# A first MLP tile of 768 tokens in two parts that share each chunk of weights

## The chip, the cores and the metric

The kernel runs on 1 core of one Trainium2 chip. The metric is the device time of one execution in microseconds. The core's engines are TensorE (PE; PEld in the profile is its weight load), VectorE (DVE), ScalarE (ACT), GpSimd (POOL) and SyncE (SP), each with a queue of instructions that it works through in order; matmul results go to PSUM, which has 8 banks of 128 x 512 fp32.

## The reference

All is fp32. Attention with a decay bias over 8 batches, 8 heads, 576 positions; then, on its output x, a Fourier mixing, a layer norm and an MLP of 512 to 2048 to 512:

```python
scores = q @ k.T / sqrt(D); bias = -(cum[:, None] - cum[None, :])   # cum: running sum of max(s, 0)
scores = where(causal, -1e9, scores + minimum(bias, 0))
x = softmax(scores) @ v                       # heads side by side: [8, 576, 512]
u = x + real(fft(fft(x, axis=1), axis=2))     # over positions, then over features
un = (u - mean(u)) / sqrt(var(u) + 1e-6)
out = u + relu(un @ w_ch1) @ w_ch2            # 512x2048, 2048x512
```

## The kernel before

**Attention.** The 32 pairs of heads (8 batches of 4) go through a loop, `for i in range(NP)`, in which the steps of several pairs are woven together: scores of pair i, `av` of pair i - 1, `recip` and `finish` of pair i - 2. `recip` sends the softmax sums through DRAM and back as a broadcast `rb`; `finish` multiplies and, for half of the pairs, moves the result into `xs` by DMA. When a batch's four pairs are finished, `folds` adds and subtracts mirrored halves on DVE, ACT and POOL, and `fourier` does the mixing in matmuls (pzs, pzc, pyc, pys, p), adds it to xa and xs and writes u to a DRAM buffer `uD`. The Fourier buffers are the pool `fft`.

**The MLP.** The 4608 tokens are cut into 9 tiles of 512 (`TOK`), with features on the partitions. `ln_tile` (L127 on) loads u, takes mean and variance by matmuls with a matrix of ones (`spread_sum`), and leaves the centred values as a rounded high part `uch` and a low part `ucl`, with `mu` and the reciprocal `r` of the deviation. `mlp_tile` (L164 on) goes over 16 chunks f of 128 hidden features. A chunk takes 12 matmuls into a PSUM tile h (`uch` and `ucl` against the chunk's high and low weights wh and wl, L183), a relu that is evicted as zh (ACT, L187) and zl (DVE, L188), and 12 matmuls into four accumulators acc0 to acc3 (L196 to L198), which are issued one chunk later. The tile's outputs are scaled and added up on DVE and POOL through three `o` buffers and one `w` (L204 to L212) and written (L213).

**The weights.** They come as 8-byte floats. `rounded` (L74 on) makes fp32 out of 256 columns in four DVE operations, one ACT and one POOL operation; `load_w` (L101 on) then splits them into wh and wl. Chunks 0 to 5 are converted during attention and parked in DRAM (`wD`); 6 to 15 are converted while the first MLP tile runs, by the generator `rest`, from which `mlp_tile` pulls two chunks ahead and which `ahead` also advances. Chunks 0 to 2 lie in the pool `w0`, 3 to 7 in `w1`, and 8 to 15 in `wB`, which takes the place of the Fourier buffers: `rest` first runs the last batch's mixing to its end and closes `fft`. After that all 16 chunks stay in SBUF for the other 8 tiles.

**Order.** `weave` interleaves generators: it advances the one whose progress (what it has yielded over its total) is smallest. PE keeps the traced order as long as the context `order` is open; for the other engines, and for PE after `order.close()`, the scheduler of the language sets each queue's order at build time, with the traced order as priority.

**PSUM.** `ps` has 3 banks, which `bank` hands out in turn for h, scores, Fourier and sums; `psm` has 5 for attention, and when attention ends `accp` takes four for acc0 to acc3.

**Around the first tile** the order traced is: `av` of the last pair woven with batch 6's mixing, the first tile's layer norm and the loads of chunks 0 to 2; `recip` and `finish` of the last pair; `folds` of the last batch; then the first tile, woven with `fourier` of the last batch and `ahead`. The second tile's layer norm follows with a delay of 9 steps.

Of the kernel before, what the change touches and what calls it, by code (L numbers as in the profile page):

```python
# [8 lines left out]
F32 = mybir.dt.float32  # L9
F32R = mybir.dt.float32r  # L10
AF = mybir.ActivationFunctionType
ALU = mybir.AluOpType
# [14 lines left out]
TOK = 512  # L27
NC = 6
# [13 lines left out]
def fused_kernel(ctx, tc, qkT, vA, sP, wP, tabD, tabS, corr, out):  # L42
# [84 lines left out]
    def ln_tile(t0, n, lag):  # L127
# [10 lines left out]
        mlp = mlps[t0 // TOK % 2]  # L138
        mu = mlp.tile([128, TOK], F32, tag="mu", name="mu")
        nc.scalar.copy(mu[:, :n], pm[:, :n])  # L140
        uch = mlp.tile([128, 4, TOK], F32R, tag="uch", name="uch")
        ucl = mlp.tile([128, 4, TOK], F32R, tag="ucl", name="ucl")
# [14 lines left out]
        r = mlp.tile([128, TOK], F32, tag="r", name="r")  # L157
# [6 lines left out]
    def mlp_tile(t0, n):  # L164
        uch, ucl, mu, r = LN.pop(t0)
        last = t0 + n == NT
        if last:
            w = lnp.tile([128, 4, TOK], F32, tag="u", name="u")
            for j in range(4):
                nc.gpsimd.tensor_add(w[:, j, :n], uch[:, j, :n].bitcast(F32), ucl[:, j, :n].bitcast(F32))  # L170
                nc.gpsimd.tensor_add(w[:, j, :n], w[:, j, :n], mu[:, :n])
        acc = [accp.tile([128, TOK], F32, tag=f"acc{j}", name=f"acc{j}") for j in range(4)]
        held = []
        for f in range(NF + 1):
            if f < NF:
                while min(f + 2, NF) not in W and next(feed, None) is not None:
                    pass
                wh, wl = W[f]
                h = bank("h")
                i = 0  # L180
                for a, b in ((wh, uch), (wl, uch), (wh, ucl)):
                    for j in range(4):
                        nc.tensor.matmul(h[:, :n], a[:, j * 128:(j + 1) * 128], b[:, j, :n], start=i == 0, stop=i == 11)  # L183
                        i += 1
                zh = zp.tile([128, TOK], F32R, tag="zh", name="zh", bufs=2)
                zl = zp.tile([128, TOK], F32R, tag="zl", name="zl", bufs=2)
                nc.scalar.activation(zh[:, :n], h[:, :n], AF.Relu)  # L187
                nc.vector.scalar_tensor_tensor(out=zl[:, :n], in0=h[:, :n], scalar=0.0, in1=zh[:, :n].bitcast(F32), op0=ALU.max, op1=ALU.subtract)  # L188
            if f < NF:
                held.append((wh, wl, zh, zl, f))  # L190
            if f and not (last and f == NF - 1):
                steps = [(x, j) for x in range(len(held) if f == NF else 1) for j in range(4)]
                for x, j in sorted(steps, key=lambda s: 2 * s[0] + s[1]):
                    a, b, y, z, g = held[x]
                    cs = slice(512 + j * 128, 512 + (j + 1) * 128)
                    nc.tensor.matmul(acc[j][:, :n], a[:, cs], y[:, :n], start=g == 0, stop=False)  # L196
                    nc.tensor.matmul(acc[j][:, :n], b[:, cs], y[:, :n], start=False, stop=False)  # L197
                    nc.tensor.matmul(acc[j][:, :n], a[:, cs], z[:, :n], start=False, stop=g == NF - 1)  # L198
                del held[0]
            if f < NF:  # L200
                yield 1.0
        for j in range(4):
            o = op.tile([128, TOK], F32, tag="o", name="o", bufs=3)
            nc.vector.tensor_mul(o[:, :n], r[:, :n], acc[j][:, :n])  # L204
            if last:
                nc.vector.tensor_add(w[:, j, :n], w[:, j, :n], o[:, :n])
                o = w[:, j]
            else:
                w = op.tile([128, TOK], F32, tag="w", name="w")
                nc.gpsimd.tensor_add(w[:, :n], uch[:, j, :n].bitcast(F32), ucl[:, j, :n].bitcast(F32))  # L210
                nc.gpsimd.tensor_add(w[:, :n], w[:, :n], mu[:, :n])
                nc.gpsimd.tensor_add(o[:, :n], o[:, :n], w[:, :n])  # L212
            (nc.scalar if last and j % 2 else nc.sync).dma_start(out=out[j, :, t0:t0 + n], in_=o[:, :n])  # L213

# [132 lines left out]
    psm = attb_ctx.enter_context(tc.tile_pool(name="psm", bufs=5, space=PSUM))  # L347
# [229 lines left out]
    tiles = [(t, min(TOK, NT - t)) for t in range(0, NT, TOK)]  # L577
# [7 lines left out]
    for i in range(NP):  # L585
# [26 lines left out]
        if i == NP - 1:  # L612
# [3 lines left out]
            norm = ln_tile(*tiles[0], 6)  # L616
# [3 lines left out]
        if i >= 7 and i % 4 == 3:  # L620
# [17 lines left out]
    accp = ctx.enter_context(pool("accp", space=PSUM))  # L638
    order.close()
# [25 lines left out]
    for x, (t0, n) in enumerate(tiles):  # L665
        streams = [[mlp_tile(t0, n), NF]]
        if x == 0:
            streams.append([chain(idle(1000), mixing), FOURIER * 0.6])
            streams.append([ahead(), 100])
        if x + 1 < len(tiles):  # L670
            streams.append([later(ln_tile(*tiles[x + 1], 1), 4 if x else 9), 12])
        weave(*streams)
# [140 lines left out]
```

## Time and profile before

| | |
|---|---|
| median of 3 runs | 1427.62 us (1426.01 to 1429.96) |
| the profiled execution: time, span | 1426.1 us, 1424.4 us |
| mean granted TensorE clock | 0.971 |
| busy: PE, DVE, ACT, POOL | 1305.1, 745.7, 539.3, 561.6 us |
| first MLP matmul, first matmul of the second tile | at 572.44, at 702.47 us |
| DMA | 125.05 MB, 88 GB/s in the mean |

Times are from the start of the span. A row of the timeline has the start, the length, the engine, the line, the operation, its tiles (out<-in), shapes and count; in square brackets stands the idle time before it and what ended that. Recorded lengths of matmuls overlap, since they are pipelined: what one costs in a row of them is read from start to start. A row by stretch has the stretch, its length, and the busy time of PE, PEld, DVE, ACT and POOL with their counts, then the granted clock, the share of DMA and GB/s. A row of the groups has the line, engine, operation, tiles, shapes and count, then busy us and mean ns of one, then the idle time before.

### The profile page before, as it was taken

The page shows a single profiled execution, that of the slowest core. Times are in us where ns is not written, and L with a number is a line of the kernel's source. Part 1 is how long each engine was busy: PE and PEld are TensorE (multiplying, and loading weights), DVE is VectorE, ACT ScalarE, POOL GpSimd, SP SyncE. Part 2 cuts the span into 40 slices and gives each one's busy share as a digit, 9 for nine tenths or more (in the row PEclk, how much of TensorE's full clock was granted, in tenths as well). Part 3 has the DMA queues.
Part 4 walks back from the last instruction along what each step waited for, and adds up shares of the span by engine and source line. Part 5 has one row for each costly group of instructions (what it writes and reads, how often), then busy time and mean ns, then how long its engine had stood idle before and what let it go on. Part 6 is the DMA issues. An engine that isn't in the chain of part 4 may idle for free.

```text
span 1424.4 us, 17997 instructions
## 1 busy us (share of the span) xinstructions
PE 1305.1 (92%) x6190; PEld 1068.7 (75%) x6190; DVE 745.7 (52%) x1684; ACT 539.3 (38%) x1211; POOL 561.6 (39%) x543
## 2 busy tenths in 40 slices
PE   4887979897988887997899999999999999999998
PEld 3766868686777676775688888888888888888886
DVE  6667677877777788799833233222332223322212
ACT  4775756676665656344321121211212112121110
POOL 6445465656546566565720402204022040123300
PEclk9998999999999997999899999999999999999999
DMA  8555556565655555433200000000000000000000
GB/s 214 156 159 144 163 149 180 158 168 159 159 161 144 166 149 163 162 123 121 79 8 30 31 30 15 15 30 31 30 15 15 30 30 30 15 16 0 30 0 30
DMA packets 78230, 125.05 MB, mean 88 GB/s; under 512 B 11256, under 2 KB 36249, under 8 KB 78139
## 3 DMA queue, kind: packets, MB, share of 16 engines
q1 hardware_dynamic: 75627, 119.83, 28.4%
q0 software_dynamic: 1696, 2.50, 0.9%
q10 hardware_dynamic: 816, 1.57, 0.3%
q8 instruction: 49, 0.80, 0.2%
q14 instruction: 42, 0.34, 0.1%
HBM read 76.85 MB, written 23.07 MB: 70 GB/s over the span
## 4 chain that ended last, share of the span: by engine, by line
PE 51%; DVE 7%; POOL 2%; DMA 1%; issue 1%; ACT 1%; SPq 0%; DVEq 0%; POOLq 0%; ACTq 0%
PE h L183 25%; PE acc L198 8%; PE acc L196 8%; PE acc L197 8%; POOL we L89 1%; DVE wm L88 1%; DVE we L83 1%; DVE wm L85 1%; DVE we L87 1%; DVE wl L114 1%; ACT wh L112 1%; DMA wl<-wD 0%; POOL wl L114 0%; DVE ucl L148 0%; DVE zl L188 0%
## 5 line engine op out<-in xcount | busy, mean ns | idle before, releaser
L188 DVE SCALAR_TENSOR_TENSOR zl<-h,zh 128x512 fp32r<-128x512 f32 x144 | 98.6, 686 | 405.5 <-ACT zh L187 405.4
L187 ACT ACTIVATE zh<-h 128x512 fp32r<-128x512 f32 x144 | 85.9, 596 | 530.1 <-PE h L183 530.1
L198 PE MATMUL acc<-zl,wh 128*128 128x512 f32 x576 | 227.5, 396 | 4.9 <-DVE zl L188 4.9
L196 PE MATMUL acc<-zh,wh 128*128 128x512 f32 x576 | 227.6, 395 | 1.0 <-ACT zh L187 1.0
L197 PE MATMUL acc<-zh,wl 128*128 128x512 f32 x576 | 226.8, 394 | 0.0
L523 PE MATMUL pavB<-P,va 128*128 128x320 f32 (+2 forms) x640 | 189.1, 389 | 9.5 <-ACT stage L527 8.9
L459 PE MATMUL pm<-KQ 128*128 128x256 f32 (+3 forms) x384 | 156.5, 427 | 44.4 <-DVE Mx L466 23.1
L495 ACT ACTIVATE P<-ps 128x320 f32<-128x320 f32 (+4 forms) x384 | 145.9, 393 | 110.5 <-PE ps L492 106.8
L491 PE MATMUL ps<-KQ 128*128 128x256 f32 (+2 forms) x384 | 154.1, 404 | 24.4 <-ACT P L495 14.0
L183 PE MATMUL h<-uch,wh 128*128 128x512 f32 x576 | 159.9, 398 | 8.3 <-ACT wh L112 8.3
L183 PE MATMUL h<-uch,wl 128*128 128x512 f32 x576 | 158.1, 396 | 0.8 <-DVE wl L114 0.8
L183 PE MATMUL h<-ucl,wh 128*128 128x512 f32 x576 | 156.9, 393 | 0.0
L466 DVE CUSTOM_DVE_ANT_0 trash<-pm,amask 128x128 bf16<-128x128 f32 (+3 forms) x256 | 123.5, 482 | 34.2 <-PE pm L459 16.9
L212 POOL TENSOR_TENSOR o<-o,w 128x512 f32<-128x512 f32 x32 | 41.8, 1305 | 252.3 <-issue 218.5
L183 PEld LDWEIGHTS h<-uch,wh 128*128 128x128 f32 x576 | 108.2, 190 | 35.9 <-ACT wh L112 12.1
L198 PEld LDWEIGHTS acc<-zl,wh 128*128 128x128 f32 x576 | 108.7, 189 | 32.0 <-DVE zl L188 6.9
L183 PEld LDWEIGHTS h<-uch,wl 128*128 128x128 f32 x576 | 109.2, 190 | 26.6 <-DVE wl L114 1.2
L196 PEld LDWEIGHTS acc<-zh,wh 128*128 128x128 f32 x576 | 108.6, 188 | 26.1 <-ACT zh L187 1.8
L183 PEld LDWEIGHTS h<-ucl,wh 128*128 128x128 f32 x576 | 108.9, 189 | 24.7
L197 PEld LDWEIGHTS acc<-zh,wl 128*128 128x128 f32 x576 | 108.6, 189 | 24.7
L459 PEld LDWEIGHTS pm<-KQ 128*128 128x128 f32 x384 | 78.4, 207 | 64.7 <-DVE Mx L466 30.2
L492 PE MATMUL ps<-q,k 128*128 128x256 f32 (+2 forms) x384 | 120.5, 316 | 3.1 <-POOL q L438 3.1
(140 smaller groups left out, 2066.9 us busy)
## 6 DMA issues: line engine op xcount, KB each, us to landing
qk<-in_qkT_dram SPq DMA_DIRECT2D x32, 576.0 KB
raw<-in_wP_dram SPq DMA_DIRECT2D x64, 256.0 KB
va<-in_vA_dram SPq DMA_DIRECT2D x32, 480.0 KB
q<-KQ SPq DMA_DIRECT2D x32, 288.0 KB
k<-KQ SPq DMA_DIRECT2D x32, 288.0 KB
rb<-rd SPq DMA_DIRECT2D x64, 144.0 KB
u<-uD SPq DMA_DIRECT2D x8, 1024.0 KB
out_dram<-o SPq DMA_DIRECT2D x32, 256.0 KB
```

Of the source, the lines that this page charges most:

```text
L183: nc.tensor.matmul(h[:, :n], a[:, j * 128:(j + 1) * 128], b[:, j, :n], start=i == 0, stop=i == 11)
L187: nc.scalar.activation(zh[:, :n], h[:, :n], AF.Relu)
L188: nc.vector.scalar_tensor_tensor(out=zl[:, :n], in0=h[:, :n], scalar=0.0, in1=zh[:, :n].bitcast(F32), op0=ALU.max, op1=ALU.subtract)
L196: nc.tensor.matmul(acc[j][:, :n], a[:, cs], y[:, :n], start=g == 0, stop=False)
L197: nc.tensor.matmul(acc[j][:, :n], b[:, cs], y[:, :n], start=False, stop=False)
L198: nc.tensor.matmul(acc[j][:, :n], a[:, cs], z[:, :n], start=False, stop=g == NF - 1)
L459: nc.tensor.matmul(p[:, :n], qy[:, h, 128 * c:128 * c + 128], ky[:, h, k0:k0 + n], start=True, stop=True)
L466: nc.vector.tensor_tensor_reduce(out=trash[:nq, :n], in0=p[:nq, :n], in1=amask[:nq, m0:m0 + n], scale=1.0, scalar=first if x else NEG, op0 ...
L491: nc.tensor.matmul(p[:, :n], ky[:, h, ksl], qy[:, h, a:a + n], start=True, stop=False)
L492: nc.tensor.matmul(p[:, :n], k1[:, h, ksl], q1[:, h, a:a + n], start=False, stop=True)
L495: nc.scalar.activation(P[:, o:o + a + n - lo], p[:, lo - a:n], AF.Exp, scale=0.125)
L523: nc.tensor.matmul(p[:, a - lo:n], va[:, c, vs], P[:, o:o + w], start=c == 0, stop=c == cs[-1])
```

## The change

Tile 0 now has two parts: tokens 0 to 511, and `EXTRA` = 256 more (512 to 767) that use the same chunk of weights two chunks later (`LAG`). The tiles behind it are seven of 512, and a last one of 256. `mlp_tile` takes a list of parts; the work of one chunk of one part is moved into `chunk`, and the output into `write`, without a change in its operations.

The second part has its own `mu`, `uch`, `ucl`, `r` in the pool `mlp0`, its own zh and zl in a pool `zx`, and two PSUM banks `accx`, each of which holds two accumulators of 256 columns. So in tile 0 PSUM holds acc (4 banks), accx (2) and `ps1` (2 banks for h, Fourier and sums, where 3 stood). After tile 0, accx is closed and `ps2` takes its two banks; `bank` then alternates between both pools.

`order.close()` moves ahead of the last pair's `recip` and `finish`, and the first chunk of tile 0 is traced there, with the second part's layer norm; the last batch's `folds` are traced within tile 0, right ahead of `fourier`, behind the third step. The last constant shrinks the SBUF space that is set aside for the descriptors of DMAs issued by POOL, which are the loads of the Fourier tables alone.

```diff
+EXTRA = 256
...
-    ps = ctx.enter_context(tc.tile_pool(name="ps", bufs=3, space=PSUM))
+    ps_ctx = ExitStack()
+    banks = [ps_ctx.enter_context(tc.tile_pool(name="ps", bufs=3, space=PSUM))]
     def bank(name):
-        return ps.tile([128, 512], F32, tag="bank", name=name)
+        banks.append(banks.pop(0))
+        return banks[-1].tile([128, 512], F32, tag="bank", name=name)
...
+    LAG = 2
-    def mlp_tile(t0, n):
+    def mlp_tile(parts):
+        last = sum(parts[-1]) == NT
+        part = []
+        for x, (t0, n) in enumerate(parts):
+            if x:
+                two = [accx.tile([128, 512], F32, tag=f"accx{j}", name=f"accx{j}") for j in range(2)]
+                acc = [two[j // 2][:, 256 * (j % 2):256 * (j % 2) + 256] for j in range(4)]
+            else:
+                acc = [accp.tile([128, TOK], F32, tag=f"acc{j}", name=f"acc{j}") for j in range(4)]
+            part.append(dict(t0=t0, n=n, x="x" if x else "", w=EXTRA if x else TOK, lag=LAG * x, acc=acc, held=[]))
+        for g in range(NF + 1 + LAG * (len(parts) - 1)):
+            if g < NF:
+                while min(g + 2, NF) not in W and next(feed, None) is not None:
+                    pass
+            for p in part:
+                f = g - p["lag"]
+                if 0 <= f <= NF:
+                    chunk(p, f, last)
+            if g < NF:
+                yield 1.0
+        for p in part:
+            yield from write(p, last)
...
-    tiles = [(t, min(TOK, NT - t)) for t in range(0, NT, TOK)]
+    tiles = [[(0, TOK), (TOK, EXTRA)]] + [[(t, min(TOK, NT - t))] for t in range(TOK + EXTRA, NT, TOK)]
...
+    ps_ctx.close()
+    accp = ctx.enter_context(pool("accp", space=PSUM))
+    banks[:] = [ctx.enter_context(tc.tile_pool(name="ps1", bufs=2, space=PSUM, reuse_waits="tile"))]
+    accx_ctx = ExitStack()
+    accx = accx_ctx.enter_context(pool("accx", space=PSUM))
+    zx = ctx.enter_context(pool("zx"))
+    order.close()
+    b = NB - 1
+    feed = iter(())
+    first = mlp_tile(tiles[0])
     recip(NP - 1)
-    finish(NP - 1)
-    b = NB - 1
-    weave([folds(b, *xbuf[b]), 1.0])
-    mixing = fourier(b, *xbuf.pop(b))
+    weave([ln_tile(*tiles[0][1], 2), 10], [take(first, N0 - 2), 1], [later(call(finish, NP - 1), 1), 10])
     attb_ctx.close()
...
-    accp = ctx.enter_context(pool("accp", space=PSUM))
-    order.close()
+    folding = folds(b, *xbuf[b])
+    mixing = chain(folding, fourier(b, *xbuf.pop(b)))
...
-    for x, (t0, n) in enumerate(tiles):
-        streams = [[mlp_tile(t0, n), NF]]
+    for x, parts in enumerate(tiles):
+        streams = [[mlp_tile(parts) if x else first, NF]]
         if x == 0:
             streams.append([chain(idle(1000), mixing), FOURIER * 0.6])
             streams.append([ahead(), 100])
+        if x == 1:
+            accx_ctx.close()
+            banks.append(ctx.enter_context(tc.tile_pool(name="ps2", bufs=2, space=PSUM, reuse_waits="tile")))
...
-    nc = bacc.Bacc("TRN2", target_bir_lowering=False, num_devices=1)
+    nc = bacc.Bacc("TRN2", target_bir_lowering=False, num_devices=1, dynamic_dma_scratch_size=4096)
```

More of the change, by code (lines that the diff above doesn't have):

```diff
@@ L162, in fused_kernel @@
     LN, W = {}, {}
-    def mlp_tile(t0, n):
[L165 to L168, printed above, removed]
-            for j in range(4):
[L170 to L201, printed above, removed]
@@ L202, in mlp_tile, with write @@
+    def write(p, last):
+        t0, n, acc = p["t0"], p["n"], p["acc"]
+        uch, ucl, mu, r = p["ln"]
         for j in range(4):
@@ L213, in mlp_tile @@
             (nc.scalar if last and j % 2 else nc.sync).dma_start(out=out[j, :, t0:t0 + n], in_=o[:, :n])
+        yield 0.0
     fft_ctx = ExitStack()
@@ L615, in fused_kernel @@
             mlps = [ctx.enter_context(pool("mlp0"))]
-            norm = ln_tile(*tiles[0], 6)
+            norm = ln_tile(*tiles[0][0], 6)
             streams.append([take(norm, 10), 10 / 0.9])
```

51 lines of the change are left out of this document (42 added, 9 removed).

## The prediction

> **What bounds the kernel now.** I read the page's slices first, then busy time by stretch, then what TensorE waited for in the first MLP tile, then that tile in order of time.
>
> ```profile
> PE 1305.1 (92%) x6190; PEld 1068.7 (75%) x6190; DVE 745.7 (52%) x1684; ACT 539.3 (38%) x1211; POOL 561.6 (39%) x543
> PE   4887979897988887997899999999999999999998
> DVE  6667677877777788799833233222332223322212
> ...
> PEclk9998999999999997999899999999999999999999
> ```
>
> A slice is 35.6 us. From slice 20 on TensorE is full and VectorE idles: there only fewer matmul columns would help. Slices 16 to 19 (570 to 712 us) are the other way round, VectorE full and TensorE not. That is the first MLP tile, whose chunks of weights are still being made from their 8-byte form. By stretch (busy us and count of PE, PEld, DVE, ACT, POOL; PE clock; DMA):
>
> ```profile
> 640.00:688.00 48.00, 37.44 (x139) 26.50 (x139) 46.60 (x110) 23.76 (x53) 26.30 (x31) 0.95 0.33 110
> 688.00:703.00 15.00, 11.76 (x35) 8.68 (x35) 12.83 (x16) 5.27 (x10) 12.15 (x10) 0.73 0.21 70
> 572.44:702.47 130.03, 110.92 (x473) 85.38 (x472) 116.56 (x247) 56.13 (x125) 77.47 (x84) 0.95 0.36 122
> 702.47:1418.80 716.33, 716.30 (x3102) 582.43 (x3100) 205.91 (x269) 125.73 (x213) 154.76 (x115) 1.00 0.06 22
> ...
> PE h L183 <- ACT wh L112: 8.3, 8, 1.7
> PE acc L198 <- DVE zl L188: 4.9, 4, 2.7
> ...
> DVE xr L559 <- DMA rb<-rd: 3.0, 1, 3.0
> DVE Aw L251 <- DMA xs<-xr: 2.1, 1, 2.1
> ```
>
> Behind the stretches stand waits: two of TensorE in 572 to 703 (us in total, times, longest) and two of VectorE in 572 to 640. TensorE waits for the next chunk's wh, and for a zl that stands behind weight work in VectorE's queue. VectorE is busy 46.60 of 48 us while TensorE issues 139 matmuls. The price of TensorE's work in that tile:
>
> ```profile
> 711.64 1.10 PE L183 MATMUL h<-uch,wh 128*128 128x512 f32 x4
> 717.20 1.10 PE L183 MATMUL h<-uch,wh 128*128 128x512 f32 x4
> ...
> 608.23 0.87 PE L284 MATMUL pzs<-dsin,Do 128*96 128x256 f32 x6
> 608.93 0.88 PE L292 MATMUL pzc<-dcos,De 128*96 128x258 f32 x6
> ...
> 618.18 1.37 PE L315 MATMUL pys<-ssin,zs 96*128 96x290 f32 x9
> 619.39 1.35 PE L336 MATMUL p<-scos,z 97*4 97x290 f32 x9
> ```
>
> Start to start (717.20 - 711.64), a 512-token chunk of 24 matmuls is 5.56 us when nothing waits, so 16 are 89. Six 256-wide matmuls are 0.70 us, 117 ns each; nine 290-wide ones 1.21 us. The last batch's Fourier part (three pzs at 0.70, three pzc at about 0.84, five groups at 1.2) is 10.6 us. With 0.5 of sums the tile is 100 us of work in 130.0: **30 us lost**. That is all that can be filled here.
>
> **The change part by part.**
>
> *256 tokens move from the MLP's steady part into the first tile.* Steady, before: 8 tiles in 716.33 us, 89.54 each. After: 7 tiles, 626.8, and one of 256 tokens: 384 matmuls at 117 ns and 0.5 of sums, 45.4; together 672.2. **Saved behind the first tile: 44.1 us.** The narrow price with whole 128x128 weights, from attention:
>
> ```profile
> 543.90 0.28 PE L492 MATMUL ps<-q,k 128*128 128x256 f32 x1
> 544.02 0.28 PE L491 MATMUL ps<-KQ 128*128 128x256 f32 x1
> 544.14 0.28 PE L492 MATMUL ps<-q,k 128*128 128x256 f32 x1
> ```
>
> Start to start 120 ns, and each has its own weight load: at 0.12 instead of 0.117 the two narrow halves cost 2 x 384 x 0.003 = 2.3 us more, the upper bound; below lies 5.56/48 = 116 ns.
>
> *The first tile gets that work.* Its TensorE floor is 100 + 45.4 = 145.4 us, so from the same start (572.44; nothing traced ahead of it changes) it ends at 717.8 at the earliest, against 702.47.
>
> *What VectorE gains in work before the last weights.* The 256-token zl of 16 chunks, and the layer norm of these tokens, which used to be part of a late tile. Rows (the first two give the price of a 256-wide eviction, start to start; the last is from the groups of 640 to 688):
>
> ```profile
> 596.34 0.41 DVE L70 TENSOR_TENSOR zs<-pzs,zs 96x256 fp32r<-96x256 f32 x1
> 596.67 0.67 DVE L188 SCALAR_TENSOR_TENSOR zl<-h,zh 128x512 fp32r<-128x512 f32 x1
> ...
> 705.37 3.35 DVE L159 RECIPROCAL r<-r 128x512 f32<-128x512 f32 x1 [2.03 <-ACT r L158]
> ...
> L148 DVE TENSOR_TENSOR ucl<-u,uch 128x512 fp32r<-128x512 f32 x1 | 0.7, 684 | 0.0
> ```
>
> A 256-wide eviction is 0.33 us: 16 are 5.3. The norm has 14 VectorE operations at half of 0.684 and a reciprocal at half of 3.35: 6.5. So **12 us** more. Against that, VectorE idled 13.5 of the 130 us, 5.1 of them for the last pair's transfers (the waits for rb and xs above); the weight work now stands ahead of the fold and can fill that. The last chunk's wl was written by 693 (POOL's row in the next fence); now about 700 by VectorE's work alone.
>
> *The fold moves behind three chunks, the last Fourier part with it.* Its VectorE, ScalarE and POOL work and its row transfer (SP) are only reordered against weight work, cost 0 in sum. But weights 8 to 15 lie where the Fourier buffers were:
>
> ```profile
> 624.02 1.01 ACT L112 CAST wh<-we 128x256 fp32r<-128x256 f32 x3
> ...
> 691.61 1.44 POOL L114 TENSOR_TENSOR wl<-we,wh 128x256 fp32r<-128x256 f32 x2
> ```
>
> Wh of chunk 8 came at 624.0, 3.4 us behind the end of the Fourier matmuls begun at 619.39 (1.2 us long). All Fourier matmuls are traced ahead of chunk 6 in both kernels. TensorE now has ahead of that point six wide chunks (33.4), four narrow (11.2) and 10.6, with some 5 us of waits for weights 3 and for the fold: from 572.4 to 633, and wh of chunk 8 at about 636 instead of 624. From there to the last wl it took 693 - 624 = 69 us for 8 chunks; with 8 x 0.33 it is 72, so the last weights come at **708**. This is the later of the two, and I take it.
>
> *The drain.* At 708 chunk 15 of the wide part starts. Behind it TensorE has 24 + 12 wide matmuls (8.3 us) and, two chunks behind, 7 narrow groups of 12 (9.8): the first tile ends at **726**. Between 717.8 (TensorE never waits) and 740 (each of the 8 late chunks is paced at 10.5 rather than 9 us because VectorE also waits for TensorE) this is what I take.
>
> *A new wait behind it.* The wide part's four output tiles and the narrow part's four pass through three o buffers and POOL:
>
> ```profile
> 701.52 1.27 POOL L210 TENSOR_TENSOR w<-uch,ucl 128x512 f32<-128x512 f32 x1
> 702.88 1.62 POOL L211 TENSOR_TENSOR w<-w,mu 128x512 f32<-128x512 f32 x1
> 704.58 1.29 POOL L212 TENSOR_TENSOR o<-o,w 128x512 f32<-128x512 f32 x1
> ```
>
> A wide one is 4.2 us of POOL, a narrow one 2.1. The wide part is done five narrow groups, 7 us, before the narrow one. The first two narrow o get a buffer when wide outputs two and three have left, about 3 x 4.2 = 12.6 us behind the wide part's end, the other two some 4 us later: the narrow accumulators are emptied about 5 and 10 us after the tile's end. They now lie in banks that the second tile's second and fourth h want, 2.8 and 14 us after its start. I take **2 us**, between 0 and 8 (POOL as slow as a late start makes it).
>
> *PSUM.* h, narrow h, Fourier and sums share 2 banks where 3 stood; priced in the 5 us of waits above and as a rival. *Bytes:* the 256-token u load is issued where a 512-token one was; the second tile's load moves behind it and has 100 us. *The smaller descriptor space* concerns only POOL's table loads:
>
> ```profile
> L292 PE MATMUL pzc<-dcos,De x144: 276/282/531, 147.2 to 613.8; 128*96 128x258 f32 x96, 128*97 128x258 f32 x48
> L234 POOL DMA_DIRECT2D dcos<-in_tabD_dram x2: 734/838/943, 10.8 to 22.5; - x2
> ```
>
> Issued by 22.5, first read at 147: over 100 us hide it.
>
> *The end.* The last tile's writes halve:
>
> ```profile
> 1418.37 0.40 PE L198 MATMUL acc<-zl,wh 128*128 128x512 f32 x1
> ...
> 1420.68 0.69 DVE L206 TENSOR_TENSOR u<-u,o 128x512 f32<-128x512 f32 x1
> ```
>
> From the last matmul to the end of the span (1424.4) are 6 us of halved operations and transfers: 1.5 us saved, between 0 and 3.
>
> **Sum**, against the profiled execution (span 1424.4, time 1426.1; the median of three is 1427.62, 1.5 above): -44.1 + (726 - 702.5) + 2 - 1.5 = -20.1 us. From the median that is 1407.5; I say 1408.
>
> **The rivals.**
>
> *Half hidden.* VectorE and TensorE, now both nearly full, wait for each other in their fixed orders. End of the first tile 736 to 745: the gain is 10 to 1 us, 1418 to 1427. For it: the 97% of VectorE above. Against: a narrow chunk adds 0.33 to some 8.7 us.
>
> *The change does nothing.* The first tile grows by all of 44 to 46 us, as if its 30 us could not be filled: 1425 to 1430. Against: TensorE's waits are for weights, and the narrow matmuls need no others.
>
> *Slower: two banks.* A chunk's zl reads its bank late:
>
> ```profile
> 637.02 1.09 PE L183 MATMUL h<-uch,wh 128*128 128x512 f32 x4
> 639.82 0.40 PE L196 MATMUL acc<-zh,wh 128*128 128x512 f32 x1
> ...
> 647.42 0.50 PE L198 MATMUL acc<-zl,wh 128*128 128x512 f32 x1 [1.38 <-DVE zl L188]
> ```
>
> The h begun at 637.02 ended at 639.8, and the acc that needs its zl waited to 647.4: 7.5 us. If the next wide h must wait for that, its bank being the only one, a chunk takes 2.8 + 7.5 = 10.3 us: 572.4 + 16 x 10.3 + 7 (narrow drain) + 10.6 = 755, hence 1434. It decides from 10.1 us a chunk. Against: the lag is TensorE running ahead; held back, it shortens.
>
> *Slower: weight loads of narrow matmuls not hidden.* The split makes 384 more loads and 768 matmuls are narrow. Were each paced by its recorded load of 190 ns, not 117, 768 x 0.073 = 56 us come on top of my forecast: 1464. Against: the 120 ns spacing above, with full weights.
>
> ```profile
> L183 PEld LDWEIGHTS h<-uch,wl 128*128 128x128 f32 x576 | 109.2, 190 | 26.6 <-DVE wl L114 1.2
> ```
>
> [...]
>
> **How the numbers follow.** Forecast (first tile ends 717 to 736, 1396 to 1418) 0.72; half hidden 0.14; nothing 0.06; two banks 0.05; narrow loads 0.03. 0.3% (4.3 us, so below 1423.3) is about what a measurement of this kernel can tell. Faster takes the forecast and over half of half hidden: 0.81. Same: the rest of that, and nothing: 0.11. Slower: the last two, 0.08. The range goes from 1396 (717.8, no new wait, 3 us at the end: -44.1 + 15.3 - 3 = -31.8) to 1423, inside half hidden; outside lie the last three cases and two fifths of that one, 0.2.
>
> **What the profile after would show.** Narrow acc and h at about 117 ns start to start; matmuls in 640 to 690 close to 100% and the clock at 1.0; wh of chunk 8 near 636, the last wl near 708, the second tile's first h near 726; the steady tiles still 89.5 us. Wrong if the last wl comes past 720, if chunks in the first tile are spaced over 10 us, or if h of the second tile waits over 8 us for a narrow accumulator.

## The result, and the profile after

The changed kernel takes **1443.66 us** (median of 4 runs, 1443.22 to 1447.59) against 1427.44 us before in the same runs (1426.01 to 1429.96): a ratio of 1.0118 (95% interval 1.0095 to 1.0141). It is slower by some 17 us; 1408 was forecast, with a range to 1423. The profiled execution has a span of 1442.2 us (1424.4 before).

The page of the changed kernel, busy shares by slice and the granted clock:

```profile
PE   4987989797998988878889999999999999999998
DVE  6667677767777778968742323223332233321222
...
PEclk9998989999989998999998999999999999999999
```

Slices are 36.1 us. The first MLP tile used to be four slices with VectorE nearly full (7, 9, 9, 8, then a 3). Now VectorE falls to 4 while that tile still runs (slice 20, 721 to 757 us), and TensorE is at 8, 7, 8, 8, 8 through it (slices 16 to 20): the tile is longer and *both* engines have more room in it.

In the new kernel h of chunk 0 stands ahead of batch 6's last Fourier group, so "from the first h" would compare unlike things. All stretches below start where that last group (`pys`) starts, which I call the **mark**: 571.23 before, 573.17 after. The first MLP tile is cut there, at the end of the last batch's Fourier part, at the last wl, and at the second tile's first h. After, by stretch (PE, PEld, DVE, ACT, POOL busy; clock; DMA), the fourth row being all that follows:

```profile
573.17:642.99 69.82, 55.54 (x299) 46.97 (x297) 54.37 (x113) 25.30 (x60) 32.13 (x33) 0.90 0.32 114
642.99:717.80 74.81, 63.93 (x343) 54.07 (x340) 60.48 (x143) 31.71 (x75) 41.92 (x51) 0.95 0.33 108
717.80:763.70 45.90, 37.92 (x221) 33.63 (x222) 19.43 (x29) 9.54 (x20) 19.80 (x17) 0.91 0.12 42
763.70:1442.20 678.50, 673.72 (x3101) 556.07 (x3099) 194.53 (x270) 118.92 (x213) 140.68 (x116) 1.00 0.06 22
```

The kernel before, cut at the same three points:

```profile
571.23:619.39 48.16, 42.86 (x218) 35.08 (x217) 39.68 (x88) 19.65 (x45) 25.26 (x27) 1.00 0.42 144
619.39:692.30 72.91, 62.35 (x248) 46.65 (x246) 68.14 (x151) 32.64 (x75) 45.56 (x53) 0.95 0.34 114
692.30:702.47 10.17, 6.93 (x19) 4.86 (x18) 9.24 (x10) 4.25 (x8) 7.86 (x7) 0.73 0.25 83
```

The tile went from 131.2 us (48.2 + 72.9 + 10.2) to 190.5 (69.8 + 74.8 + 45.9): **59.3 us more for 45.4 of work, of which some 22 should have fallen into gaps** (the forecast let the tile grow by 23.5). TensorE's gaps (length less busy) were 5.3, 10.6 and 3.2 us; now they are 14.3, 10.9 and 8.0. Not one got smaller. Behind the tile nearly all is as forecast: from the second tile's first h to the end of the span 678.5 us (1442.2 - 763.70) against 721.9, 43.4 saved for the 45.6 of the forecast (44.1 in the tiles and 1.5 at the end).

What TensorE waited for between the mark and the second tile:

```profile
PE h L209 <- DVE zl L215: 13.2, 7, 3.1
PE accx L225 <- DVE zl L215: 7.4, 1, 7.4
PE var L126 <- ACT th L72: 6.1, 1, 6.1
PE pzs L315 <- DVE zl L215: 5.1, 1, 5.1
```

The old waits of that tile, 8.3 us of h for wh and 4.9 of acc for zl, are gone. These four stand in their place. An h reads no zl: when it waits for one, it waits for its PSUM bank, which an earlier zl has yet to read. The timeline shows each (in square brackets the wait):

```profile
584.50 0.58 PE L126 MATMUL var<-th,ones 128*128 128x256 f32 x1 [6.12 <-ACT th L72]
...
619.49 1.60 PE L315 MATMUL pzs<-dsin,Do 128*96 128x256 f32 x6 [5.06 <-DVE zl L215]
...
648.51 0.70 ACT L115 CAST wh<-we 128x256 fp32r<-128x256 f32 x2
...
672.22 1.20 PE L209 MATMUL h<-uch,wh 128*128 128x512 f32 x4 [2.84 <-DVE zl L215]
...
684.04 2.07 PE L209 MATMUL h<-uch,wh 128*128 128x512 f32 x4 [3.09 <-DVE zl L215]
...
708.68 1.20 PE L209 MATMUL h<-uch,wh 128*128 128x512 f32 x4 [2.17 <-DVE zl L215]
...
717.16 0.73 POOL L117 TENSOR_TENSOR wl<-we,wh 128x256 fp32r<-128x256 f32 x1 [0.52 <-ACT wh L115]
...
757.12 1.26 POOL L136 TENSOR_TENSOR t<-u 128x512 f32<-128x512 f32 x1
758.42 1.73 DVE L138 TENSOR_TENSOR t<-t,t 128x512 f32<-128x512 f32 x1 [5.83 <-POOL t L136]
760.08 0.41 DVE L215 SCALAR_TENSOR_TENSOR zl<-h,zh 128x256 fp32r<-128x256 f32 x1
760.54 0.58 PE L225 MATMUL accx<-zl,wh 128*128 128x256 f32 x1 [7.42 <-DVE zl L215]
...
763.70 1.91 PE L209 MATMUL h<-uch,wh 128*128 128x512 f32 x4
```

At 584.50 the narrow part's own norm stands at the head of TensorE's queue, and chunk 1 behind it. From 672.22 (chunk 9) to 708.68 (chunk 12) a wide chunk takes 12.2 us where its matmuls and the narrow ones need 8.4. At 758.42 a step of the *third* tile's norm on VectorE has waited 5.83 us for POOL, whose addition for it stood behind the wide outputs until 757.12; the last narrow zl stands behind that step, and TensorE behind the zl. Last wl at 717.16, second tile 46.5 us later.

### The profile page after: what moved, and what is told of

Same layout as the page of the kernel before. It is cut to its first block, busy times and chain, and to the rows that moved or that the text cites. A ratio compares the mean times of both kernels' runs of the same rounds, so it can differ in the third digit from the quotient of the medians.

```text
span 1442.2 us, 18880 instructions
## 1 busy us (share of the span) xinstructions
PE 1314.3 (91%) x6578; PEld 1097.6 (76%) x6578; DVE 745.4 (52%) x1719; ACT 542.8 (38%) x1239; POOL 559.6 (39%) x557
## 4 chain that ended last, share of the span: by engine, by line
PE 50%; DVE 7%; POOL 3%; DMA 1%; ACT 1%; issue 1%; DVEq 0%; POOLq 0%; ACTq 0%
PE h L209 24%; PE acc L225 8%; PE acc L223 8%; PE acc L224 8%; POOL we L92 1%; DVE we L86 1%; DMA raw<-in_wP_dram 1%; DVE we L90 1%; DVE wm L91 1%; DVE zl L215 1%; DVE wm L88 1%; DVE wl L117 1%; ACT wh L115 0%; DVE u L149 0%; POOL o L242 0%
## 5 line engine op out<-in xcount | busy, mean ns | idle before, releaser
L215 DVE SCALAR_TENSOR_TENSOR zl<-h,zh 128x512 fp32r<-128x512 f32 (+1 forms) x160 | 101.3, 634 | 404.4 <-ACT zh L214 404.0
L214 ACT ACTIVATE zh<-h 128x512 fp32r<-128x512 f32 (+1 forms) x160 | 88.3, 553 | 529.2 <-PE h L209 528.2
L223 PE MATMUL acc<-zh,wh 128*128 128x512 f32 (+1 forms) x576 | 220.1, 382 | 0.6 <-DVE yp L352 0.6
L225 PE MATMUL acc<-zl,wh 128*128 128x512 f32 (+1 forms) x576 | 219.0, 381 | 0.2 <-DVE zl L215 0.2
L224 PE MATMUL acc<-zh,wl 128*128 128x512 f32 (+1 forms) x576 | 219.1, 380 | 0.0
L209 PE MATMUL h<-uch,wh 128*128 128x512 f32 (+1 forms) x640 | 164.9, 380 | 13.9 <-DVE zl L215 13.2
L209 PE MATMUL h<-uch,wl 128*128 128x512 f32 (+1 forms) x640 | 162.1, 376 | 0.0
L209 PE MATMUL h<-ucl,wh 128*128 128x512 f32 (+1 forms) x640 | 159.9, 372 | 0.0
L242 POOL TENSOR_TENSOR o<-o,w 128x512 f32<-128x512 f32 (+1 forms) x36 | 44.6, 1238 | 264.0 <-issue 216.9
L209 PEld LDWEIGHTS h<-uch,wh 128*128 128x128 f32 x640 | 115.7, 192 | 38.8 <-DVE zl L215 15.6
## 6 DMA issues: line engine op xcount, KB each, us to landing
rb<-rd SPq DMA_DIRECT2D x64, 144.0 KB
```

The lines of the kernel that those rows point to most:

```text
L223: nc.tensor.matmul(acc[j][:, :n], a[:, cs], zh[:, :n], start=g == 0 and not (x and j % 2), stop=False)
L224: nc.tensor.matmul(acc[j][:, :n], b[:, cs], zh[:, :n], start=False, stop=False)
L225: nc.tensor.matmul(acc[j][:, :n], a[:, cs], zl[:, :n], start=False, stop=g == NF - 1 and not (x and j % 2 == 0))
```

## The experiments

Each kernel ran with runs of the kernel before beside it. Those spread from 1423 to 1438 us over the chips, so I compare ratios, and stretches from the mark, which are each from one profiled execution: **F** for the end of the Fourier part (start of its last group), **W** for the start of the last operation that writes a wl, **T** for the second tile's first h. Before: F 48.2, W 121.1, T 131.2. After: F 69.8, W 144.0, T 190.5.

**1. One suspect at a time.** The fold back in its place, right behind `finish`:

```diff
+    weave([folds(b, *xbuf[b]), 1.0])
-    folding = folds(b, *xbuf[b])
-    mixing = chain(folding, fourier(b, *xbuf.pop(b)))
+    mixing = fourier(b, *xbuf.pop(b))
```

> The changed kernel with one part undone: the last batch's folds are traced right behind the last pair's finish again, ahead of the first tile's second chunk. Three theories of where the changed kernel lost. Banks: the next wide h waits for the zl of the one before, since h, narrow h and Fourier share two banks, and that zl stands behind weight work; then earlier weights do not help, and the second tile still begins within 4 us of 763 (time 1440 to 1446). Late fold: the Fourier buffers came free 21 us later than before (wh of chunk 8 at 648.5), and VectorE idled about 17 us in 633 to 652; then wh of chunk 8 comes at about 630 and the second tile begins about 15 us earlier (time 1426 to 1432). Order (weight work traced too far ahead of zl): as banks.

Measured 1.0079 (1.0049 to 1.0109); F 67.6, T 187.9. The late fold alone is 2 us of the Fourier stretch.

Without the stream that advances the weights ahead of the matmuls (`streams.append([ahead(), 100])` removed):

> The changed kernel without the stream that advances the weights on its own, so that weight work is traced only as the tile's chunks ask for it, two ahead. Order: zl then stands nearer in VectorE's queue; wide h in 660 to 718, now 11.8 us apart, come about 9.2 apart, and the time falls by some 10 to 15 us to 1429 to 1434. Banks: without the stream the same weight work still stands between two zl; spacing stays over 11 us and the time within 4 us of 1443.7. Late fold: the spacing in 660 to 718 is not its matter; time within 4 us.

Measured 1.0086 (1.0062 to 1.0111); T 190.0, and wide chunks 9 to 12 are 12.2 us apart as in the changed kernel. The traced place of the weight work is not it.

The kernel *before* with two banks in the first tile and four afterwards:

```diff
+    banks[:] = [ctx.enter_context(tc.tile_pool(name="ps1", bufs=2, space=PSUM, reuse_waits="tile"))]
...
+        if x == 1:
+            banks.append(ctx.enter_context(tc.tile_pool(name="ps2", bufs=2, space=PSUM, reuse_waits="tile")))
```

> The kernel before with nothing changed but the PSUM banks for h, Fourier and sums from the first tile on: two instead of three in the first tile, four afterwards. Banks: a chunk's h can no longer run ahead of zl; the spacing of h in 640 to 690, 8.8 us, rises to 10.3 or more, the second tile begins at about 715 instead of 702.5, time about 1440. Late fold and order: no part of them is here; time within 3 us of the kernel before (1424 to 1431).

Measured 1.0041 (1.0016 to 1.0065); F 50.7, T 135.9. Two banks alone lengthen the tile by 4.7 us, 2.5 of it in the Fourier stretch; by the ratio they cost 6 us. That is a part, not the whole.

The first addition of the norms behind the first tile on VectorE instead of POOL:

```diff
-        nc.gpsimd.tensor_add(t[:, :n], u[:, 0, :n], u[:, 1, :n])
+        (nc.vector if t0 > TOK else nc.gpsimd).tensor_add(t[:, :n], u[:, 0, :n], u[:, 1, :n])
```

> The changed kernel with one operation moved: the first addition of a tile's layer norm runs on VectorE instead of POOL, for the tiles behind the first. In the changed kernel the last narrow zl waited in VectorE's queue behind an addition that waited 5.8 us for POOL, and TensorE stood 7.4 us. Tail: that wait goes, time about 1437. If it is only replaced by the next thing that POOL or an o buffer holds: 1442 to 1445.

Measured 1.0090 (1.0059 to 1.0121). The wait at accx fell from 7.4 to 1.9 us and T to 183.6, but the rest took 682.4 us instead of 678.5: half of it came back, 2.2 us as a wait of acc for zl.

**2. VectorE's queue.** Counting the first operations of weight slices (four make a chunk) between one wide zl and the next tells how far the weights run ahead. A row has the stretch, its length, busy time and count of that one operation, then the clock, the share of DMA and GB/s. After, four stretches from 658.20 on, and before, from 661.60 on:

```profile
658.20:671.40 13.20, 2.19 (x7) 1.00 0.31 103
671.40:683.30 11.90, 3.79 (x6) 1.00 0.36 121
683.30:695.50 12.20, 2.14 (x5) 0.86 0.35 120
695.50:707.90 12.40, 1.92 (x6) 0.86 0.37 117
```

```profile
661.60:669.50 7.90, 1.99 (x4) 1.00 0.37 129
669.50:678.10 8.60, 1.13 (x4) 0.90 0.37 122
```

Before: four slices to a chunk, in step. After: five to seven (an operation on the edge of two rows counts in both), so zl waits behind more than a chunk's conversion and TensorE waits for zl with chunks already converted. This run (without the ahead stream) holds the weight work of chunk f back until zl of chunk f - 3 is issued:

```diff
-        nc.vector.tensor_scalar(e, hi, 0x7FF00000, None, op0=ALU.bitwise_and)
+        with tc.issue_after(ZL[f - BEHIND].ins) if f - BEHIND in ZL else ExitStack():
+            nc.vector.tensor_scalar(e, hi, 0x7FF00000, None, op0=ALU.bitwise_and)
+            nc.vector.tensor_scalar(m, hi, 0xFFFFF, 0x100000, op0=ALU.bitwise_and, op1=ALU.bitwise_or)
...
```

> The changed kernel without the stream that advances the weights, and with an edge of issue order (no wait) that queues the VectorE work of weight chunk f behind the zl of the wide chunk f - 3. In the changed kernel VectorE's queue holds 5 to 7 slices of weight work (a chunk is 4) between two wide zl, which the next wide h waits for; before it held 3 or 4. Build order (the queue's order, made at build time, lets weight work run ahead, and TensorE idles now for weights that it needs only later): the spacing of wide h in the converting stretch falls from 11.8 to about 9.4 us, and the way from the ninth h to the second tile shrinks by about 9 us; time about 1434. Banks alone: a wide h still waits some 8 us for its bank, spacing over 11 us, time as the changed kernel's (1441 to 1446).

Measured 1.0093 (1.0062 to 1.0124). Chunks 9 to 12 went from 12.2 to 10.4 us apart, but W came at 148.6 instead of 144.0, and T at 185.9 instead of 190.0 without the edges. In step or not, the stretch is nearly the same: what zl gains, the weights lose.

**3. Half the width.** 128 extra tokens, accx in one bank, three banks for h (four in all behind), and the same with two:

```diff
-EXTRA = 256
+EXTRA = 128
...
+                one = accx.tile([128, 512], F32, tag="accx", name="accx")
+                acc = [one[:, 128 * j:128 * j + 128] for j in range(4)]
...
+    banks[:] = [ctx.enter_context(tc.tile_pool(name="ps1", bufs=3, space=PSUM, reuse_waits="tile"))]
```

> The changed kernel with 128 tokens in the second part instead of 256. Its four accumulators then fit one PSUM bank, and the bank that comes free goes to h, Fourier and sums: three in the first tile. Compare with the next run, which leaves that bank empty. Banks: the stretch from the first h to the seventh, where the last Fourier part lies, shrinks by about 14 us (what two banks cost the kernel before), and a wide h no longer waits for zl; time 1420 to 1430, 15 to 20 under the next run. Build order: only the Fourier stretch gains, since weight work still stands ahead of zl (up to 7 slices); 10 to 14 us under the next run.

> As the run before with 128 tokens and one bank of accumulators for the second part, but two banks for h, Fourier and sums as in the changed kernel; one bank stays empty. All theories: 1436 to 1446, and 10 to 20 us over the run with three banks. If the two agree within 4 us, banks are not what costs.

Measured 1.0328 (1.0299 to 1.0358) and 1.0365 (1.0341 to 1.0390): far worse, which I had not expected. Matmuls of 128 columns in the run with three banks, twelve of them from 726.78:

```profile
726.78 0.28 PE L223 MATMUL accx<-zh,wh 128*128 128x128 f32 x1
...
728.01 0.28 PE L225 MATMUL accx<-zl,wh 128*128 128x128 f32 x1
```

Eleven intervals in 1.23 us: **112 ns each, against 120 for twice the columns.** From 256 to 128 columns a matmul with its own weights hardly gets cheaper, so 128 tokens cost the first tile 43 us (384 x 0.112), while the rest took 706.6 us, 15 less than before. T was 188.6 with three banks, 199.7 with two. Three banks took h's wait for zl from 21.7 to 2.9 us, and waits of acc and accx for zh and zl, 3.2 us with two banks, grew to 16.7: most of the wait moves to the next reader of the same queues. By the ratios the third bank is worth 5 us, not the 11 of T.

**4. The narrow part later.** Fold behind `finish`, the narrow part six chunks behind, its norm inside the tile, and its two banks lent to h and the Fourier part until it starts (the stream that advances the weights is left out here and in experiment 5); with the edges of experiment 2, then without them, then at ten and at seventeen chunks (wholly behind the wide part):

```diff
-    LAG = 2
+    LAG = 6
...
+    banks.append(psa_ctx.enter_context(tc.tile_pool(name="psa", bufs=2, space=PSUM, reuse_waits="tile")))
...
+        if not f and p["x"]:
+            p["acc"] = narrow_acc()
```

> The edge of issue order of the run with weights behind zl, and three more edits: the folds are traced ahead of the first tile's second chunk again; the narrow part follows six chunks behind (LAG 6) instead of two; until it starts its two accumulator banks belong to h, Fourier and sums (four banks), and its layer norm is traced within the first tile. If banks cost in the Fourier stretch and build order in the converting stretch, both go: the seventh h begins about 50 us behind the first (78 in the changed kernel, 48 before), wide h in the converting stretch are about 9.4 us apart, the second tile begins about 160 us behind the first h instead of 196: time 1405 to 1412, under both kernels. If the cost is the work itself (VectorE's, with a narrow part, fills the tile whatever the order): 1430 or more.

> The changed kernel with the fold right behind finish, the narrow part six chunks behind the wide one instead of two, its layer norm traced inside the first tile, and the two banks of the narrow accumulators lent to h and the Fourier part until the narrow part starts. Stretches are taken from the start of the last Fourier group of batch 6: to the second tile's first h it was 131 us before the change and 190 after it. Theory 1 (narrow work that stands ahead of the end of the weights' conversion delays the conversion and waits in TensorE's queue behind the wide h; the work itself is cheap): Fourier over at about 55 instead of 70, second tile at 172 to 184, 1422 to 1436. Theory 2 (the 45 us of narrow work, its evictions and its norm cost some 59 us wherever they stand in the tile): 187 to 193, 1437 to 1444.

> The same with the narrow part ten chunks behind. Before the change TensorE ran chunks 6 to 10 back to back and waited only for chunks 11 to 15, 2 to 3.5 us at each, so narrow work that starts at chunk 10 meets nothing but those waits. Theory 1: conversion as before the change (last wl at 120 to 127 us of the stretch), about 14 of the 45 us hidden, second tile at 162 to 172, 1411 to 1422: faster than both. Theory 2: 187 to 193, 1437 to 1444.

> The same with the whole narrow part behind the wide one: nothing of it overlaps the conversion. Theory 1: first tile as before the change plus 45 us of narrow work, second tile at 174 to 183, what stands behind it 44 us less, 1423 to 1432: about the time before, and 12 to 20 us under the changed kernel, so that overlap at two chunks' distance is worse than none. Theory 2: 187 to 193, 1437 to 1444.

| | ratio (interval) | F | W | T |
|---|---|---|---|---|
| 6, with edges | 1.0075 (1.0040 to 1.0110) | 55.2 | 136.7 | 184.9 |
| 6 | 1.0108 (1.0081 to 1.0135) | 55.3 | 136.3 | 189.3 |
| 10 | 1.0077 (1.0053 to 1.0101) | 55.2 | 134.9 | 187.2 |
| 17 | 1.0156 (1.0126 to 1.0186) | 55.2 | 136.3 | 195.5 |

My theory had the narrow work's early place as the cause; it fell. With *all* narrow matmuls behind the wide ones the last weights still came 15 us later than before. That run (17), by stretch, and three groups of its narrow norm on VectorE in these two stretches:

```profile
576.07:631.26 55.19, 46.93 (x219) 39.24 (x218) 43.31 (x91) 21.99 (x54) 30.78 (x30) 0.88 0.37 127
631.26:713.00 81.74, 64.99 (x249) 47.12 (x246) 75.62 (x163) 35.71 (x79) 46.23 (x54) 0.94 0.33 108
...
L151 DVE TENSOR_TENSOR ucl<-u,uch 128x256 fp32r<-128x256 f32 x4 | 3.8, 939 | 0.0
L149 DVE TENSOR_TENSOR u<-u,mu 128x256 f32<-128x256 f32 x4 | 2.8, 718 | 0.0
L162 DVE RECIPROCAL r<-r 128x256 f32<-128x256 f32 x1 | 1.7, 1739 | 0.0
```

VectorE is busy 118.9 us up to the last weights, against 107.8 before (39.68 + 68.14 in the rows above): 11 us are added work; for the rest it idles. The 11 are nearly all the narrow norm: these nine operations take 8.3 us, and with its sums and their splitting it comes to 10.6, where 6.5 were forecast. (Of the weight work one operation, wm<-raw, is 5.0 us slower than before, 574 ns in the mean for 449; the fold and other steps are faster by about as much.) The changed kernel's overlap (T 190.5) saves 5 us against none at all.

**5. The moved order.** As at ten chunks, but `recip`, `finish` and fold traced ahead of the tile and of `order.close()`, as before the change; then also the wide outputs written at once and the second tile's two POOL additions on VectorE; then that order at a distance of two:

```diff
+    recip(NP - 1)
+    finish(NP - 1)
+    weave([folds(b, *xbuf[b]), 1.0])
...
+    order.close()
-    weave([take(first, N0 - 2), 1], [later(call(finish, NP - 1), 1), 10])
```

> As e10_lag_10, but recip, finish and the fold of the last pair are traced as before the change, ahead of the first tile and of order.close. Stretches from the start of batch 6's last Fourier group, as they were before the change: Fourier over at 48, last wl at 120, second tile at 131; with e10_lag_10 55, 135 and 187. If the moved order is what delays the conversion: Fourier over at 48 to 51, last wl at 122 to 130, second tile at 175 to 182, 1425 to 1433. If it is the narrow part's own work (its norm and evictions on VectorE) wherever the fold stands: last wl at 132 to 137, second tile at 184 to 190, 1436 to 1443.

> As e12_order_before_lag_10, and the wide part's outputs are written as soon as its accumulators are done (while the narrow part goes on), and the first addition of the second tile's layer norm is on VectorE instead of POOL, so that no zl of the narrow part stands in VectorE's queue behind an operation that waits for POOL. If that queue is what holds TensorE up at the tile's end (5.9 to 8.6 us at accx in the runs so far): the wait gone, second tile 5 to 8 us earlier than in e12_order_before_lag_10, 1420 to 1428, the best version of this change. If something else is late next there: under 3 us.

> As e12_order_before_lag_10 with the narrow part two chunks behind, as in the changed kernel (its norm is traced at once, the two banks are lent only until it starts). Against the changed kernel (Fourier over at 70, last wl at 144, second tile at 190) it undoes the moved order alone. If the moved order is what cost: Fourier over at 56 to 62, last wl at 130 to 136, second tile at 176 to 182, 1427 to 1433. If narrow work in front of the Fourier part costs, and weight work ahead of zl: 66 to 71, 140 to 145, 185 to 191, 1437 to 1444.

| | ratio (interval) | F | W | T |
|---|---|---|---|---|
| distance 10 | 1.0053 (1.0034 to 1.0072) | 53.5 | 130.5 | 184.2 |
| 10, early write | 1.0040 (1.0019 to 1.0062) | 51.2 | 128.9 | 181.7 |
| distance 2 | 1.0056 (1.0033 to 1.0080) | 64.4 | 137.8 | 175.3 |

The last row undoes the moved order (and lends the two banks until the narrow part starts, two chunks in, and traces the narrow norm inside the tile), and halves the loss: 1.0118 to 1.0056. F, W and T come 5, 6 and 15 us earlier; 6 of the 15 are lost again behind (the rest takes 684.4 us). The wait at accx is gone in all three, so the early write had nothing left to remove; its moved additions are the second tile's, while the wait of the changed kernel came from the third's. None of them reaches the kernel before.

**6. Without the late weights.** Chunks 8 to 15 use the weights of chunks 0 to 7, in the changed kernel and in the one before:

```diff
         for f in range(N1, NF):
-            yield from load_w(wB, f)
+            W[f] = W[f - N1]
+            yield 1.0
```

> The changed kernel without the conversion of chunks 8 to 15: these chunks use the weights of chunks 0 to 7 again (so their part of the sums is left out and another stands in its place). VectorE has no weight work then behind chunk 7. If the weight work in VectorE's queue is what paces the wide h at 11.8 us: spacing 8.3 to 8.5 us (5.6 + 2.8, TensorE full) from chunk 6 on, no wait of h for zl there, second tile at 163 to 172 us behind the start of batch 6's last Fourier group (190 in the changed kernel). If the two banks that a wide and a narrow h share pace it: spacing stays at 10 to 12 us, second tile at 183 to 195.

> The kernel before, chunks 8 to 15 again with the weights of chunks 0 to 7. Fourier over at 48 us as before, chunks 6 to 15 at 5.6 us each, second tile at 104 to 109 us (131 before). The difference of e15_no_late_weights to this run is the price of the narrow part where no conversion disturbs: 45.5 us of TensorE's work, and what the longer Fourier stretch (15 to 21 us) and the wait at the narrow accumulators (7 us) cost beside it: 57 to 66.

Measured 0.9956 (0.9929 to 0.9983) and 0.9823 (0.9759 to 0.9887), 1425.61 and 1406.17 us. The changed kernel without late weights: two stretches from the mark, three waits, and h of chunks 9 to 11:

```profile
577.51:646.87 69.36, 55.03 (x298) 46.82 (x297) 47.75 (x95) 23.95 (x57) 29.65 (x30) 0.90 0.26 92
646.87:751.40 104.53, 96.41 (x563) 85.39 (x561) 27.64 (x45) 16.32 (x33) 24.09 (x22) 0.96 0.09 30
```

```profile
PE accx L225 <- DVE zl L215: 7.5, 1, 7.5
PE var L126 <- ACT th L72: 6.1, 1, 6.1
...
PE h L209 <- DVE zl L215: 2.4, 2, 1.8
```

```profile
673.05 1.09 PE L209 MATMUL h<-uch,wh 128*128 128x512 f32 x4
...
689.73 1.09 PE L209 MATMUL h<-uch,wh 128*128 128x512 f32 x4
```

The kernel before without them:

```profile
580.56:628.57 48.01, 44.50 (x218) 37.28 (x218) 35.44 (x76) 18.51 (x42) 24.37 (x27) 0.94 0.33 112
628.57:687.80 59.23, 59.23 (x267) 48.87 (x265) 18.58 (x28) 11.61 (x20) 9.71 (x11) 1.00 0.11 38
```

This settles the spacing: same two banks, and chunks are 8.34 us apart ((689.73 - 673.05) / 2), h's wait for zl 2.4 us instead of 13.2. Behind the Fourier part the two banks need the weight work in VectorE's queue to hurt. It also splits the loss. Late weights cost the kernel before 24.0 us (131.24 - 107.28) and the changed one 16.6 (190.53 - 173.93): **the narrow work filled 7 us of the 24**; by the ratios, 25 and 23 us, it filled still less, but with two runs of the kernel before without late weights their interval is some 9 us either way. And with no late weights at all the change costs 19.4 us: the Fourier stretch is 21.4 us longer (9.9 of it narrow matmuls) and the wait at accx is there with its 7.5 us. **So these losses do not need the conversion of chunks 8 to 15, behind which most of the narrow work was to hide.** Chunks 6 and 7 are still converted in the Fourier stretch of both runs, so what that work adds there is not taken out.

## Why the prediction was wrong

*What held.* The saving behind the tile: to the last matmul 42.3 us for 44.1 (715.9 from 702.47 to 1418.37, 673.6 from 763.70 to 1437.31), and behind it 1.1 for 1.5. The narrow price, in the timeline of the changed kernel, from the first to the last of twelve narrow accx matmuls:

```profile
679.35 0.28 PE L223 MATMUL accx<-zh,wh 128*128 128x256 f32 x1
...
680.67 0.28 PE L225 MATMUL accx<-zl,wh 128*128 128x256 f32 x1
```

Eleven intervals in 1.32 us are 120 ns each, the upper bound of the forecast. The weight loads were hidden: those of the same twelve are recorded with 0.19 us each and start 120 ns apart too (PEld, 679.23 to 680.55). The bytes and the descriptor space, which show nowhere. From wh of chunk 8 to the last wl: 68.7 us (717.16 - 648.51) for 72.

*What failed* is the first tile, in two steps; the second tile's first h came at 763.7 instead of 726, 37.7 later (28.5 and 12.5 of the two steps, less the 3.3 that the late weights took under their forecast).

1. **The drain, 18 us forecast, 46.5 measured: 28.5 of the 37.7.** The step took TensorE to be level with the weights when the last ones come, with chunk 15 left. It had three wide chunks (13 to 15, and acc of chunk 12) and five narrow ones (and accx of a sixth) left, some 35 us at 232 and 120 ns a matmul, and then the 7.4 us at accx. I had filled the gaps by arithmetic: 30 us free, 23.5 more than the old end. But in the trace the narrow matmuls of a step stand behind the wide h in TensorE's queue, and none ran in the waits in front of it (2.84 us at 672.22, 3.09 at 684.04, 2.17 at 708.68). They also give VectorE one more eviction that TensorE waits for. The old waits for wh (8.3) and zl (4.9) became waits of h for zl (13.2, of which 2.4 stay without late weights).
2. **Wh of chunk 8, 636 forecast, 648.5 measured: 12.5.** "Cost 0 in sum, only reordered" was wrong. The forecast had 5 us of waits in this stretch; the trace has the norm's var at the queue's head (6.1), pzs behind a zl (5.1), and a granted clock of 0.90 instead of 1.00. VectorE idles 15.4 of the 69.8 us (54.37 busy): with the Fourier buffers in use the next weights have no place to go. The order restored, with the banks lent and the norm inside the tile, gives back 5.4 (experiment 5); with the narrow matmuls out of the way as well F is 51.2 to 53.5, still 3 to 5 over the 48.2 of before.

The pause in the weights shows in VectorE's timeline: between these two rows it starts no slice for 25 us. Before, the pause was 11.4 us, from 616.28 to 627.70.

```profile
626.84 0.28 DVE L86 TENSOR_SCALAR we<-raw 128x256 int32<-128x256 int32 x1
...
652.02 1.23 DVE L86 TENSOR_SCALAR we<-raw 128x256 int32<-128x256 int32 x3
```

The new wait was looked for at the second tile's h (2 us, up to 8); there is none. It came one place earlier, at the narrow part's own accx, through VectorE's queue and POOL, which the forecast had as the delay of the *outputs* only.

*The rivals.* "Half hidden" named the mechanism (two engines waiting for each other in fixed orders) and priced it at 10 to 19 us of the tile where it is 38. "Two banks" had the sign and nearly the time (1434), and its condition came true: chunks more than 10.1 us apart. Its reason came true in part: h's wait for zl, 13.2 us, is a wait for its bank. But two banks alone cost 4.7 us of the tile (experiment 1), and without late weights that wait falls to 2.4 us with the same two banks (experiment 6). Of the three signs that were to show the forecast wrong one came: chunks over 10 us apart. The last wl at 717 missed its 720, and h of the second tile waits for nothing.

VectorE's added 12 us were no gain to hide either: 11 are there in the run with everything narrow behind, mostly the norm at 10.6 for 6.5, and its idle time up to the last weights grew (13.3 to 18.0 us) instead of taking them up.

Open: why the norm's narrow operations cost more than half of the wide ones (a ucl of 256 columns 939 ns in the run with everything narrow behind, where half of 684 was forecast); every run with a narrow part has the norm. Open too is how norm, banks and order share the longer Fourier stretch, since they overlap there.

## What to carry to other kernels

Idle time of an engine with an in-order queue is not a store to be spent: ask, gap by gap, which instruction stands at the queue's head and whether the new work stands in front of it or behind. Price added work at every queue that it enters, small steps too: a norm of a few matmuls at the head of TensorE's queue, and one zl behind a VectorE step that waits for POOL, were waits of 6 and 7 us, each about what the overlap gained. And where a kernel is cut differently, test it once with the suspected bottleneck taken out: here the change lost about as much without the late weights (19 us) as with them (17).

## What the runs showed of the hardware

*Matmuls of 512, 256 and 128 columns.* Start to start, with a new weight tile each: 232 ns at 512 columns (5.56 us for 24), 120 at 256, 112 at 128. At 256 columns loads overlap with matmuls: in the changed kernel a load is recorded with 0.19 us, and a load and a matmul start every 120 ns (679.23 to 680.67). What keeps the spacing at 112 ns with half the columns, no run shows.

*The clock after a wait.* Five stretches of the changed kernel: behind the 6.12 us wait; between the waits of 2.84 and 3.09, and behind the latter; one that begins with the wait of 1.98 (in front of the h at 696.28), and the one behind it.

```profile
584.50:588.50 4.00, 4.00 (x10) 2.91 (x11) 2.82 (x2) 0.47 (x1) 0.98 (x1) 0.50 0.93 342
...
672.00:684.00 12.00, 8.72 (x48) 7.43 (x48) 11.93 (x27) 5.55 (x14) 6.67 (x9) 1.00 0.40 131
684.00:688.00 4.00, 3.96 (x10) 3.17 (x11) 4.00 (x11) 1.72 (x5) 1.52 (x2) 0.57 0.25 83
...
694.28:697.70 3.42, 1.44 (x7) 1.20 (x7) 3.38 (x11) 2.37 (x6) 1.42 (x2) 1.00 0.40 138
697.70:701.11 3.41, 3.41 (x10) 2.66 (x9) 3.38 (x7) 1.23 (x4) 2.53 (x4) 0.50 0.35 113
```

In the 4 us behind the waits of 6.12 and 3.09 us the granted clock is 0.50 and 0.57. My estimate from these two rows: some 2 us lost each time, so that the wait of 3.09 us cost 5. The length of the wait alone does not decide it: after 2.84 us the clock stays at 1.00, but after 1.98 us it falls to 0.50 for 3.41 us, 1.4 us after the wait is over. The trace's steps of the clock at 581.64, 588.47, 619.19, 626.02, 684.04, 687.46, 697.70 and 701.11 all lie whole multiples of 3.41 us apart, and so do those at 755.73 and 765.97. With the first tile cut into stretches of 3.41 us at these steps, the five at clock 1.00 that were followed by 0.50 have TensorE busy for 0.16, 0.00, 0.32, 1.44 and 0.81 us (from 578.22, 615.78, 680.63, 694.28 and 752.31); behind the one from 670.39, with 1.58 us busy, the clock stayed at 1.00, and so it did behind all those that were busier.
